# An H3 and SwiGLU block on one core: two groups' FFN activations of the first tokens go through DRAM, their down projection becomes seven products in the second tokens' loop

## Chip, cores and metric

One Trainium2 chip, one of its cores. The metric is the device time of one execution in microseconds (us), the median over runs. The engines are PE (TensorE), DVE (VectorE), ACT (ScalarE), POOL (GpSimd) and SP (SyncE, which here only issues DMAs). All data is float32; matmuls use float32r operands split in a high and a low part.

## The reference

2048 tokens of 512 features. A first half (a gated long convolution with a layer norm and modulation) ends in x; a second half is a SwiGLU feed-forward with 1792 hidden features:

```python
h = layernorm(x) * (1 + ca) + sa
x = x + ga * A(h, k, v, ...)             # short conv, k*v, FFT conv, gate
h = layernorm(x) * (1 + cb) + sb
x = x + gb * ((silu(h @ w_gate) * (h @ w_up)) @ w_down)
```

The change lies in the second half alone.

## The kernel before

**Tokens and features.** x stands in four blocks `xt[0..3]` of 512 tokens each. Blocks 0 and 1 are the first tokens (q = 0), 2 and 3 the second tokens (q = 1). The 1792 hidden features are 14 tiles f of 128; two tiles form a group g (7 groups).

**Gate and up.** For each (q, f), `gate_up` computes gate and up for both blocks at once as a 2 x 2 block product by seven products instead of eight (`seventh`). Each is six matmuls 128x128 by 128x512: two halves of the contraction times three passes (high and low parts). Order of products: 1, 7, 6, 2, 5, 3, 4. They go to PSUM banks a, c and b; bank a takes 1, then 6 on top, then 5, then 3, and ACT copies it out between (p1, p2, r3); bank c takes 7 and 4, b takes 2. So the next six matmuls on a bank wait for the engine that reads it. `gate_up_first` is a variant with another order (1, 5, 7, 2, 3, 6, 4) for the first step of each loop.

**Down.** For q = 0, `down` makes one of eight (block, 128-token) pieces of a group: six matmuls into a bank "dn", and DVE adds it to x. For q = 1, groups 0 to 5 use seven products too (`down_seven`): for two halves i, seven products of three matmuls. The products of one half share three banks (da, db, dc): product 1 goes to da, DVE adds da to x, then product 6 accumulates in da on top, and so on. A product that accumulates therefore waits for DVE's add of the one before. The seven operands come from hidden activations and their sums (`HOP`: A11, S3, S2, A22, A12, S1, S4), each with a high part by ACT and a low part by DVE or POOL (`hi_lo`).

**The order.** Each engine runs its instructions in the order in which the program states them. A loop over n = 2 to 27 (q = n // 14, f = n mod 14) states one `gate_up` after another. Behind its products 1, 7, 6, 2, 5, 3, 4 it calls the functions that tables `AT` and `AT2` (filled by `plan`) list for this step and product, then `feed`, which takes downs from the list `todo`; keys in the tables are product numbers. `late` holds the splits left over from the step before; `finish` states one behind each of the first three products. `SLOTS` is a table of strings that says, allocation by allocation, which buffer or PSUM bank the next tile takes.

**Work around the products in the first loop (n = 2 to 13).** `split_w` makes the seven weight operands of the next f: sums by POOL, high parts by ACT, low parts by POOL; `store_w` writes them to DRAM. `split_wd` scales w_down by gb (DVE, `wd_mul`) and splits it (ACT, POOL). `norm_stats` (DVE), `turn` (DVE 32x32 transposes), `put_rows` and `get_rows` (DMA out and in), `rows_op` and `rows_s` normalise blocks 2 and 3 and turn them so that features lie on the partitions.

**In the second loop (n = 14 to 27).** `reload_w` reads the kept weights back, one f ahead, into a second buffer. `wd_sums` scales w_down and makes its sums, `wd_seven` splits them, both in the odd step of a group.

Of the kernel before, what the change touches and what calls it, by code (L numbers as in the profile page):

```python
# [16 lines left out]
P = 128  # L17
# [25 lines left out]
def adaln_h3_swiglu(ctx, tc, q, k0, v0, kT, vT, ssm, dskip, wgu, wdn, wmod, e_fwd, e_inv, w_c, out):  # L43
# [9 lines left out]
        "e8": "501234671063724603267137537135173135157137157137105637501657305617503657",  # L53
# [3 lines left out]
        "r4": "0123401232040213210432403124031203124013420314201342031420134203142013431202143410201343120",  # L57
        "one": "456723017425036241736412506425173421750621507341573062570634170346250362417364125064251730256731546317027513643105725601341076526370140753623157047561321065745630120376546713025",
# [663 lines left out]
    def split_w(f):  # L722

        st = stage.pop(f)
        a11, a12, a21, a22 = st[:, 0, 0:2], st[:, 0, 2:4], st[:, 1, 0:2], st[:, 1, 2:4]
# [3 lines left out]
        sr = r4([P, 4, 2, P], F32, "sr")  # L729
        pool.tensor_tensor(sr[:, 0], a21, a22, op=ALU.add)  # L730
        pool.tensor_tensor(sr[:, 1], sr[:, 0], a11, op=ALU.subtract)
        pool.tensor_tensor(sr[:, 2], a11, a21, op=ALU.subtract)
        pool.tensor_tensor(sr[:, 3], a12, sr[:, 1], op=ALU.subtract)
        s = e8([P, 2, 4, 2, P], F32R, "wsum")
        act.copy(s[:, 0], sr)
        pool.tensor_tensor(
            w[:, 1, 0:2], st[:, 0].rearrange("p (a k) c -> p a k c", a=2), w[:, 0, 0:2].bitcast(F32), op=ALU.subtract
        )
        pool.tensor_tensor(w[:, 1, 2], a22, w[:, 0, 2].bitcast(F32), op=ALU.subtract)
        for i in (0, 2):  # L740
            pool.tensor_tensor(s[:, 1, i : i + 2], sr[:, i : i + 2], s[:, 0, i : i + 2].bitcast(F32), op=ALU.subtract)
        set_a(f, w, s)
# [3 lines left out]
    def store_w(f):  # L746

        w, s = AOP[f]["t"]
        kept[f] = [dp.tile(list(t.shape), F32, tag=f"{n}{f}", name=f"{n}{f}") for n, t in (("dw", w), ("ds", s))]
        for d, t in zip(kept[f], (w, s)):  # L750
            sp.dma_start(d, t.bitcast(F32))

    def reload_w(f):

        w = ffn["s"].tile([P, 2, 3, 2, P], F32R, tag="wa", name="wa", bufs=2)
        s = e8([P, 2, 4, 2, P], F32R, "wsum")
        for d, t in zip(kept[f], (w, s)):
            sp.dma_start(t.bitcast(F32), d)
        set_a(f, w, s)
# [36 lines left out]
    def wd_sums(g):  # L796

        wd_mul(g)
# [8 lines left out]
        stage["t", g] = tb  # L807

    def wd_seven(g):

        st, tb = stage.pop(("d", g)), stage.pop(("t", g))
        h = D // 2
        b22 = st[:, 1, h:]
        wb, wt = e8([P, 2, 4, h], F32R, "wdb"), e8([P, 2, 4, h], F32R, "wdt")
# [24 lines left out]
    def down(q, g, t, i):  # L839

        parts = 2 if (q, g, t, i) == (1, NG - 1, 0, 3) else 1
        for h in range(parts):
# [9 lines left out]
            if g == NG - 1:  # L852
                sp.dma_start(out[q, :, 4 * t + i, d], xv)
# [8 lines left out]
    SUM = {1: ("a", 0, 0), 7: ("c", 1, 1), 6: ("a", 1, 0), 2: ("b", 0, 0), 5: ("a", 1, 1), 4: ("c", 1, 0), 3: ("a", 0, 1)}  # L862

    def down_seven(g, i, n, bank_):

        k, t, dh = SUM[n]
        a, b = HOP[g][PROD[n][0]], WT[g][PROD[n][1]]
# [9 lines left out]
        xv = xt[2 + t][:, 2 * dh + i]  # L877
        dve.tensor_tensor(xv, xv, o, op=ALU.add)
        if i:
            slots.append(HOP[g].pop(PROD[n][0]))  # L880

    def sevens(g):
        for i in range(2):
            bank_ = {}
            todo.extend(("7", g, i, n, bank_) for n in SUM)

# [131 lines left out]
    def operand(g, n, x, e=dve):  # L1018
        h = HOP.setdefault(g, {})[n] = slots.pop(0)
        hi_lo(h, x, e)  # L1020

    def gate_up(q, f, at):

        def behind(k):
            for fn in at.get(PLACE[k - 1], ()):
                fn()
            feed(k, (q, f) == (0, G + 1))
# [28 lines left out]
        seventh(a, f, 3, True)  # L1056
        sg2 = g2("sg2")
        act.activation(sg2, a, AF.Silu)
        if sv:
# [8 lines left out]
            else:  # L1068
                dve.tensor_tensor(ra[:, 1], sg2, b, op=ALU.mult)
        else:  # L1070
# [4 lines left out]
        seventh(c_, f, 4, True)  # L1075
        dve.tensor_tensor(c_, p2, c_, op=ALU.add)
        dve.tensor_tensor(c_, sg1, c_, op=ALU.mult)
        after(q, f, c_)
# [489 lines left out]
    def release(n):  # L1568
# [31 lines left out]
    def plan(t, *steps):  # L1600
# [5 lines left out]
        (5, 1, turn, 0),  # L1606
        (5, 5, turn, 1),
        (5, 7, turn_rs),
        (5, 3, put_rows, 0),
        (5, 6, put_rs),  # L1610
        (6, 1, turn, 2),
        (6, 7, turn, 3),
        (6, 7, get_rs),
        (6, 3, put_rows, 1),
        (6, 4, get_rows, 0),
        (7, 7, get_rows, 1),
        (7, 6, rows_op, 0, 0, dve),
        (7, 4, rows_op, 1, 0, pool),
        (8, 6, rows_op, 0, 1, pool),
        (8, 6, rows_s, 0),  # L1620
        (8, 4, rows_op, 1, 1, pool),
        (9, 1, rows_s, 1),
# [136 lines left out]
```

## Time and profile before

| | us |
|---|---|
| median of 3 runs | 566.8 (566.38 to 568.26) |
| the profiled execution | 566.24 |
| its span, first to last instruction | 564.5 |
| PE busy | 552.7 |
| DVE busy | 441.5 |
| POOL busy | 317.7 |
| ACT busy | 288.7 |

The first half takes the span's first 154 us or so; the first tokens' loop runs from 173 to 347 us, the second tokens' loop to 555 us. A row of a timeline gives the start, the duration, the engine, the line in the code (always that of a helper here), the operation, result and source tiles, shapes and the count, and in brackets how long the engine stood idle before it and what ended that. A matmul's row counts its pipeline too, so six matmuls show 1.52 us while the next six start 1.36 us later.

### The profile page before, as it was taken

The numbers are of one execution on the slowest core, as the hardware profiler recorded it, in microseconds if no ns is written. First come the engines' busy times: TensorE is split into PE (matmuls) and PEld (weight loads), VectorE is DVE, ScalarE is ACT, GpSimd is POOL, SyncE is SP. The second block draws the span as 40 slices with busy tenths as digits, with TensorE's granted clock in tenths as the row PEclk, the third lists the DMA queues.
The fourth block names the chain that finished last, engine by engine and source line by source line (L and its number), as shares of the span: only waits on it lengthen the run. The fifth ranks groups of instructions, "written<-read, shape, count | busy, mean of one in ns | idle before, by whom it ended". The sixth has DMA issues, their size and how long they took to land.

```text
span 564.5 us, 9861 instructions
## 1 busy us (share of the span) xinstructions
PE 552.7 (98%) x3880; PEld 431.1 (76%) x3880; DVE 441.5 (78%) x602; ACT 288.7 (51%) x444; POOL 317.7 (56%) x298
## 2 busy tenths in 40 slices
PE   9899999898999999999999999999999999999997
PEld 9766456358788888888888888887888888888886
DVE  5989999998889666767567579858686868686766
ACT  3898889734664444434643556243434343434330
POOL 2359746899447966657978667550606061616110
PEclk9999999999999999999999999999999999999999
DMA  8998998991215655982897530544343434343304
GB/s 334 401 406 305 334 245 168 340 240 61 74 43 200 197 199 182 259 263 40 252 334 306 204 131 1 188 182 173 122 160 124 161 127 158 127 165 133 160 1 149
DMA packets 52544, 107.99 MB, mean 191 GB/s; under 512 B 19345, under 2 KB 34065, under 8 KB 46482
## 3 DMA queue, kind: packets, MB, share of 16 engines
q1 hardware_dynamic: 52498, 107.36, 56.3%
q8 instruction: 30, 0.49, 0.4%
q14 instruction: 16, 0.13, 0.1%
HBM read 72.74 MB, written 34.61 MB: 190 GB/s over the span
## 4 chain that ended last, share of the span: by engine, by line
PE 85%; DVE 9%; DMA 3%; ACT 1%; issue 1%; POOL 0%; SPq 0%; ACTq 0%; DVEq 0%
PE a L39 23%; PE dn L39 15%; PE c L39 12%; PE b L39 7%; PE da L39 6%; PE g L39 4%; PE s L39 4%; PE dc L39 3%; PE y L39 3%; DVE xs L39 3%; DVE X L39 2%; PE pk L39 2%; PE iv L39 2%; DMA er<-in_e_fwd 2%; DVE K L39 2%; PE px L39 1%
## 5 line engine op out<-in xcount | busy, mean ns | idle before, releaser
L39 PE MATMUL a<-op,wsum 128*128 128x512 f32 x432 | 109.9, 390 | 0.0
L39 PEld LDWEIGHTS a<-op,wsum 128*128 128x128 f32 x432 | 81.0, 188 | 17.5 <-ACT p L39 0.4
L39 PE MATMUL dn<-wd,acts 128*128 128x512 f32 x336 | 84.8, 389 | 0.0
L39 PEld LDWEIGHTS dn<-wd,acts 128*128 128x128 f32 x336 | 63.1, 188 | 13.1
L39 ACT COPY p<-a 128x512 f32<-128x512 f32 x50 | 29.4, 587 | 57.3 <-PE a L39 57.3
L39 DVE TENSOR_TENSOR x<-x,dn 128x512 f32<-128x512 f32 (+1 forms) x65 | 43.3, 671 | 13.2 <-PE dn L39 12.9
L39 POOL TENSOR_TENSOR wa<-ws,wa 128x512 fp32r<-128x512 f32 (+1 forms) x28 | 32.0, 1164 | 26.6 <-ACT wa L39 26.6
L39 POOL TENSOR_TENSOR tb<-wds 128x256 f32<-128x256 f32 x12 | 8.9, 744 | 62.4 <-DVE wds L39 62.4
L39 DVE TENSOR_TENSOR b<-r,c 128x512 f32<-128x512 f32 x24 | 16.7, 696 | 32.3 <-ACT sg L39 32.3
L39 ACT COPY r<-a 128x512 f32<-128x512 f32 x24 | 14.1, 587 | 53.7 <-PE a L39 53.6
L39 POOL TENSOR_TENSOR wsum<-sr,wsum 128x512 fp32r<-128x512 f32 x28 | 40.1, 1455 | 0.0
L39 PE MATMUL c<-op,wsum 128*128 128x512 f32 x156 | 39.6, 389 | 0.0
L39 PE MATMUL c<-op,wa 128*128 128x512 f32 x156 | 39.6, 389 | 0.0
L39 PE MATMUL b<-op,wa 128*128 128x512 f32 x144 | 36.5, 389 | 0.0
L39 POOL TENSOR_TENSOR wd<-wds,wd 128x512 fp32r<-128x512 f32 x14 | 18.3, 1329 | 30.4 <-ACT wd L39 30.4
L39 PEld LDWEIGHTS c<-op,wsum 128*128 128x128 f32 x156 | 29.3, 188 | 6.1
L39 PEld LDWEIGHTS c<-op,wa 128*128 128x128 f32 x156 | 29.3, 188 | 6.1
L39 POOL TENSOR_TENSOR s<-s,bcs 128x512 f32<-128x512 f32 x26 | 32.9, 1284 | 1.0
L39 DVE TENSOR_TENSOR x<-x,da 128x512 f32<-128x512 f32 x48 | 32.7, 681 | 0.9 <-PE da L39 0.9
L39 PEld LDWEIGHTS b<-op,wa 128*128 128x128 f32 x144 | 27.0, 188 | 5.6
L39 DVE TENSOR_TENSOR xs<-pk,xs 128x1024 f32<-128x1024 f32 x24 | 27.7, 1210 | 2.3 <-PE pk L39 2.2
L39 ACT ACTIVATE sg<-a 128x512 f32<-128x512 f32 x26 | 15.6, 599 | 22.5 <-PE a L39 22.5
(199 smaller groups left out, 1284.5 us busy)
## 6 DMA issues: line engine op xcount, KB each, us to landing
ds<-wsum SPq DMA_DIRECT2D x12, 1024.0 KB, 8.7
wsum<-ds SPq DMA_DIRECT2D x12, 1024.0 KB, 6.4
dw<-wa SPq DMA_DIRECT2D x12, 768.0 KB, 5.8
wa<-dw SPq DMA_DIRECT2D x12, 768.0 KB, 4.4
ws<-in_wgu SPq DMA_DIRECT2D x16, 512.0 KB, 4.3
wds<-in_wdn SPq DMA_DIRECT2D x14, 512.0 KB, 5.0
wm<-in_wmod SPq DMA_DIRECT2D x6, 1024.0 KB, 9.3
away<-X SPq DMA_DIRECT2D x3, 2048.0 KB
```

The source lines that it names most:

```text
L39: return lambda *a, **k: self.tc.keep_in_program_order(f(*a, **k))
```

## The change

For the first tokens, groups 3 and 5 (`LATER`) no longer go through `down` in the first loop. Their activations are written to DRAM (`keep_hidden`), read back in the second loop in the steps of the same group (`hidden`, n = 20, 21 and 24, 25), summed by POOL and split (`hidden_sum`, `hidden_op`), and their down is made by `down_seven` behind that of the second tokens. Those steps take two products behind each seventh, and state them ahead of the step's own DVE operations behind products 2, 5, 3 and 4 (`early`). The first tokens' downs are spread at two a step from n = 6 on.

Since `down_seven` leaves features on the partitions, blocks 0 and 1 are turned as well, with DMAs through DRAM, in n = 15 to 18, and their output is written from there.

To make room, the second loop keeps one copy of the gate and up weights: each operand of the next f is read into the place of the current one as soon as its product is stated. One of the two `wa` buffers holds w_down parts of even groups. In groups 3 and 5 the scaling and splitting of w_down move to the even step. In the first loop `split_w` is cut in three (`split_sum`, `split_a`, `split_s`), with `split_s` behind product 5 from n = 6 on; statistics, turns and row operations of blocks 2 and 3 move one step or more earlier, and their row operations and scaling go from POOL and ACT to DVE. In `SUM` products 4 and 2 change places.

The diff, without the `SLOTS` strings:

```diff
     def turn(t, i):
-        if k == 0:
+        if k == 0 and t < 2 and h:
+            nrm[t, h] = r4([P, NB * 4, 2, 32], F32, "xx")
+        elif k == 0:
             nrm[t, h] = ffn["s"].tile(...)
...
     def rows_s(t, a):
-            act.activation(d, d, AF.Identity, scale=modT[:, 1, b : b + 1], bias=modT[:, 0, b : b + 1])
+            dve.tensor_scalar(d, d, modT[:, 1, b : b + 1], modT[:, 0, b : b + 1], op0=ALU.mult, op1=ALU.add)
...
+    def split_s(f):
+        sr = stage.pop(("s", f))
+        s = e8([P, 2, 4, 2, P], F32R, "wsum")
+        act.copy(s[:, 0], sr)
+        for i in (2, 0):
+            pool.tensor_tensor(s[:, 1, i : i + 2], sr[:, i : i + 2], s[:, 0, i : i + 2].bitcast(F32), op=ALU.subtract)
+        ready(f, "S", s)
...
+    def reload_w(f, *names):
+        w, s = t = AOP[(f - 1) % NF]["t"]
...
+        wb = e8([P, 2, 4, h], F32R, "wdb") if g % 2 else stay[0]
...
-    SUM = {1: ("a", 0, 0), 7: ("c", 1, 1), 6: ("a", 1, 0), 2: ("b", 0, 0), 5: ("a", 1, 1), 4: ("c", 1, 0), 3: ("a", 0, 1)}
+    SUM = {1: ("a", 0, 0), 7: ("c", 1, 1), 6: ("a", 1, 0), 4: ("c", 1, 0), 5: ("a", 1, 1), 2: ("b", 0, 0), 3: ("a", 0, 1)}
+    LATER = (3, 5)
...
+    def keep_hidden(f, t, sg, x):
+        if f not in hid:
+            hid[f] = dp.tile([P, 2, 512], F32, tag=f"h{f}", name=f"h{f}")
+            hsum[2] = r4([P, 2, 512], F32, "hid")
+            dve.tensor_tensor(hsum[2][:, t], sg, x, op=ALU.mult)
+            return
+        dve.tensor_tensor(hsum[2][:, t], sg, x, op=ALU.mult)
+        sp.dma_start(hid[f], hsum[2])
...
-    def feed(k, hold):
-        if hold and k != 5:
+    def feed(k, q, f):
+        if not todo or (q, f) == (0, G + 1) and k != 5:
             return
-        if todo and (todo[0][0] == "7" and k > 1 or k in (2, 3, 4, 5)):
-            downs(2 if todo[0][0] == "7" and k == 5 else 1)
+        if todo[0][0] == "7":
+            if f // G in LATER:
+                downs(2 if (k, f) not in [(1, G * g) for g in LATER if g - 1 not in LATER] else 0)
+            elif k > 1 or todo[0][1] == 0 or len(todo) > 14:
+                downs(2 if k in (1, 5) else 1)
+        elif k in ((), (5,), (2, 5), (2, 4, 5), (2, 3, 4, 5))[4 if q or f < G * LATER[0] else DOWNS[f - G * LATER[0]]]:
+            downs(1)
...
     AT = {
-        (4, 7): lambda: norm_stats(2, range(0, 2)),
-        (4, 6): lambda: norm_stats(2, range(2, 4)),
+        (3, 7): lambda: norm_stats(2, range(0, 2)),
+        (3, 6): lambda: norm_stats(2, range(2, 4)),
...
+    for g in LATER:
+        n0 = NF + G * g
+        for n, k, fn, *a in (
+            (0, 5, hidden), (0, 7, hidden_sum, "S3"), (0, 2, hidden_op, "A11"), (0, 2, hidden_sum, "S1"),
+            (0, 3, hidden_sum, "S2"), (0, 6, hidden_op, "S3", pool), (1, 1, hidden_sum, "S4"),
+            (1, 1, hidden_op, "S2", pool), (1, 1, hidden_op, "A12"), (1, 5, hidden_op, "S1", pool),
+            (1, 5, hidden_op, "A22", pool), (1, 5, hidden_op, "S4", pool), (1, 5, lambda g: sevens(0, g)),
+        ):
+            also(n0 + n, k, fn, g, *a)
     for n in range(G, 2 * NF):
...
+                at[7 if n >= G * LATER[0] else 7].append(lambda nf=nf: split_sum(...))
+                at[7 if n >= G * LATER[0] else 7].append(lambda nf=nf: split_a(...))
+                at[3 if n >= G * LATER[0] else 7].append(lambda nf=nf: split_s(nf))
...
+            for e in range(NG):
+                if n == NF + G * e + (e not in LATER) - (e in LATER and e - 1 in LATER):
+                    if seven(1, G * e):
+                        at[1].append(lambda g=e: wd_sums(g))
+                        at[3].append(lambda g=e: wd_seven(g))
...
-                at[6 if n == G + 1 else 3].append(lambda g=g + 1: split_wd(g))
+                at[6 if n == G + 1 or f >= G * LATER[0] else 3].append(lambda g=g + 1: split_wd(g))
```

More of the change, by code (lines that the diff above doesn't have):

```diff
@@ L728, in split_w, with ready @@
         act.copy(w[:, 0, 2], a22)
[L729 to L736, printed above, removed]
+        e.tensor_tensor(
             w[:, 1, 0:2], st[:, 0].rearrange("p (a k) c -> p a k c", a=2), w[:, 0, 0:2].bitcast(F32), op=ALU.subtract
         )
[L739 to L742, printed above, removed]
+        e.tensor_tensor(w[:, 1, 2], a22, w[:, 0, 2].bitcast(F32), op=ALU.subtract)
+        ready(f, "w", w)
+    def ready(f, k, t):
+        stage[k, f] = t
+        if ("w", f) in stage and ("S", f) in stage:
+            set_a(f, stage.pop(("w", f)), stage.pop(("S", f)))
+    def split_w(f):
+        split_sum(f)
+        split_s(f)
+        split_a(f)
     kept = {}
@@ L750, in store_w, with resplit @@
         for d, t in zip(kept[f], (w, s)):
[L751 to L759, printed above, removed]
+            if t is s or not RESPLIT:
+                sp.dma_start(d, t.bitcast(F32))
+    def reload_w(f, *names):
+        w, s = t = AOP[(f - 1) % NF]["t"]
+        if f not in again:
+            again.add(f)
+            set_a(f, w, s)
+        for n in names:
+            if n[0] == "A" and RESPLIT:
+                i, src = {"A11": (0, wgu[f][:, 0, 0:2]), "A12": (1, wgu[f][:, 0, 2:4]), "A22": (2, wgu[f][:, 1, 2:4])}[n]
+                sp.dma_start(w[:, 1, i].bitcast(F32), src)
+                continue
+            d, x, i = (kept[f][0], w, ("A11", "A12", "A22").index(n)) if n[0] == "A" else (kept[f][1], s, int(n[1]) - 1)
+            sp.dma_start(x[:, :, i].bitcast(F32), d[:, :, i])
+    def resplit(f, n, e=pool):
+        w, i = AOP[f]["t"][0], ("A11", "A12", "A22").index(n)
+        act.copy(w[:, 0, i], w[:, 1, i].bitcast(F32))
+        e.tensor_tensor(w[:, 1, i], w[:, 1, i].bitcast(F32), w[:, 0, i].bitcast(F32), op=ALU.subtract)
+    again = set()
     def set_a(f, w, s):
@@ L807, in wd_sums @@
         stage["t", g] = tb
+    stay = []
     def wd_seven(g):
@@ L813, in wd_seven @@
         b22 = st[:, 1, h:]
-        wb, wt = e8([P, 2, 4, h], F32R, "wdb"), e8([P, 2, 4, h], F32R, "wdt")
+        if g == 0:
+            stay.append(ffn["s"].tile([P, 2, 3, 2, P], F32R, tag="wa", name="wdb0", bufs=2).rearrange("p a n k c -> p a n (k c)"))
+        wb = e8([P, 2, 4, h], F32R, "wdb") if g % 2 else stay[0]
+        wt = e8([P, 2, 4, h], F32R, "wdt")
         act.copy(wb[:, 0, 0:2], st[:, :, :h])
@@ new lines, in hidden, with hidden_sum @@
+    def hidden(g):
+        o = HOP[0, g] = {}
+        for n, fl, t, place in (("A11", 0, 0, 1), ("S1", 0, 1, 0), ("A22", 1, 1, 1), ("A12", 1, 0, 1)):
+            o[n] = slots.pop(0)
+            sp.dma_start(o[n][:, place].bitcast(F32), hid[g * G + fl][:, t])
+    def hidden_sum(g, n):
+        r = {k: v[:, 1].bitcast(F32) for k, v in HOP[0, g].items()}
+        r["A21"] = HOP[0, g]["S1"][:, 0].bitcast(F32)
+        if n == "S3":
+            hsum[0] = r4([P, 2, 512], F32, "hs")
+        if n == "S1":
+            hsum[1] = ffn["s"].tile([P, NB * 4, 2, 32], F32, tag="nn", name="hs", bufs=1).rearrange("p (a b) c d -> p a (b c d)", a=2)
+        x, y, op, at_ = {
+            "S3": ("A11", "A21", ALU.subtract, (0, 0)), "S1": ("A21", "A22", ALU.add, (1, 0)),
+            "S2": ("A22", "S3", ALU.subtract, (0, 1)), "S4": ("A12", "S2", ALU.subtract, (1, 1)),
+        }[n]
+        r["S3"] = hsum[0][:, 0]
+        if n == "S4":
+            r["S2"] = hsum[0][:, 1]
+        pool.tensor_tensor(hsum[at_[0]][:, at_[1]], r[x], r[y], op=op)
+        hraws[n] = hsum[at_[0]][:, at_[1]]
@@ L876, in down_seven, with sevens @@
             )
-        xv = xt[2 + t][:, 2 * dh + i]
+        xv = xt[2 * q + t][:, 2 * dh + i]
         dve.tensor_tensor(xv, xv, o, op=ALU.add)
+        if q == 0 and g == LATER[-1] and n in (2, 5, 4, 3):
+            sp.dma_start(out[0, :, 4 * t + 2 * dh + i], xv)
         if i:
-            slots.append(HOP[g].pop(PROD[n][0]))
-    def sevens(g):
+            slots.append(HOP[q, g].pop(PROD[n][0]))
+    def sevens(q, g):
         for i in range(2):
             bank_ = {}
-            todo.extend(("7", g, i, n, bank_) for n in SUM)
+            todo.extend(("7", q, g, i, n, bank_) for n in SUM)
     def downs(n):
@@ L939, in after @@
     def after(q, f, x):
+        if later(q, f):
+            return
         if not seven(q, f):
@@ L1026, in behind @@
                 fn()
-            feed(k, (q, f) == (0, G + 1))
+            if not ahead_(k):
+                feed(k, q, f)
         g, odd, sv = f // G, f % G, seven(q, f)
@@ L1049, in gate_up @@
         seventh(a, f, 5, True)
+        early(5)
         r3 = g2("r3")
@@ L1069, in gate_up @@
                 dve.tensor_tensor(ra[:, 1], sg2, b, op=ALU.mult)
+        elif later(q, f):
+            keep_hidden(f, 1, sg2, b)
         else:
@@ L1075, in gate_up @@
         seventh(c_, f, 4, True)
+        early(7)
         dve.tensor_tensor(c_, p2, c_, op=ALU.add)
-        dve.tensor_tensor(c_, sg1, c_, op=ALU.mult)
-        after(q, f, c_)
+        if later(q, f):
+            keep_hidden(f, 0, sg1, c_)
+        else:
+            dve.tensor_tensor(c_, sg1, c_, op=ALU.mult)
+            after(q, f, c_)
         behind(7)
@@ L1605, in adaln_h3_swiglu @@
         2,
[L1606 to L1622, printed above, removed]
+        (4, 1, turn, 0),
+        (4, 5, turn, 1),
+        (4, 7, turn_rs),
+        (4, 2, put_rows, 0),
+        (4, 2, put_rs),
+        (4, 3, turn, 2),
+        (5, 1, turn, 3),
+        (5, 1, get_rs),
+        (5, 5, put_rows, 1),
+        (5, 2, get_rows, 0),
+        (5, 6, get_rows, 1),
+        (6, 3, rows_op, 0, 0, dve),
+        (6, 4, rows_op, 1, 0, dve),
+        (7, 1, rows_op, 0, 1, dve),
+        (7, 5, rows_s, 0),
+        (7, 5, rows_op, 1, 1, dve),
+        (7, 7, rows_s, 1),
     )
@@ new lines, in adaln_h3_swiglu @@
+        (6, 4, turn, 1),
+        (6, 4, turn_rs),
+        (7, 1, put_rows, 0),
+        (7, 2, put_rs),
+        (7, 3, turn, 2),
+        (7, 4, turn, 3),
+        (8, 1, put_rows, 1),
+        (8, 6, get_rs),
+        (8, 6, get_rows, 0),
+        (8, 4, get_rows, 1),
+        (9, 4, rows_op, 0, 0, dve),
+        (10, 1, rows_op, 1, 0, dve),
+        (10, 2, rows_op, 0, 1, dve),
+        (10, 4, rows_op, 1, 1, dve),
+        (10, 6, rows_s, 0),
+        (11, 7, rows_s, 1),
+    )
+    plan(
+        1,
+        (NF + 1, 5, turn, 0),
+        (NF + 1, 5, turn, 1),
+        (NF + 1, 7, put_rows, 0),
+        (NF + 1, 7, turn, 2),
+        (NF + 1, 7, turn, 3),
+        (NF + 1, 2, put_rows, 1),
+        (NF + 1, 6, get_rows, 0),
+        (NF + 2, 5, get_rows, 1),
+    )
@@ new lines, in adaln_h3_swiglu @@
+    plan(
+        0,
+        (NF + 1, 4, turn, 0),
+        (NF + 2, 3, turn, 1),
+        (NF + 2, 4, put_rows, 0),
+        (NF + 2, 4, turn, 2),
+        (NF + 3, 5, turn, 3),
+        (NF + 3, 7, put_rows, 1),
+        (NF + 3, 2, get_rows, 0),
+        (NF + 4, 5, get_rows, 1),
+    )
+    for g in LATER:
[7 more added lines that the diff above has]
+            also(n0 + n, k, fn, g, *a)
@@ L1644, in adaln_h3_swiglu @@
     for n in range(G, 2 * NF):
         q, f = n // NF, n % NF
-        at = {k: AT2.get((n, k), []) + ([AT[n, k]] if (n, k) in AT else []) for k in range(1, 8)}
+        at = {k: [] for k in range(1, 8)}
+        if RESPLIT and n >= NF + G:
+            at[7].append(lambda f=f: resplit(f, "A22", none))
+        for k in at:
+            at[k] += AT2.get((n, k), []) + ([AT[n, k]] if (n, k) in AT else [])
         if n + 1 < 2 * NF:
@@ L1650, in adaln_h3_swiglu @@
             if n + 1 >= NF + G:
-                at[1].append(lambda nf=nf: reload_w(nf))
-            else:
-                at[7].append(lambda nf=nf: split_w(nf))
+                for k, names in ((1, ("A11",)), (7, ("S3", "S2")), (2, ("A12",)), (6, ("S1", "S4")), (4, ("A22",))):
+                    at[k].append(lambda nf=nf, names=names: reload_w(nf, *names))
+                if RESPLIT:
+                    at[2].append(lambda nf=nf: resplit(nf, "A11", none))
+                    at[4].append(lambda nf=nf: resplit(nf, "A12", none))
+            else:
+                at[7 if n >= G * LATER[0] else 7].append(lambda nf=nf: split_sum(nf, dve if later(0, nf) and 0 else pool))
+                at[7 if n >= G * LATER[0] else 7].append(lambda nf=nf: split_a(nf, dve if later(0, nf) and 0 else pool))
+                at[3 if n >= G * LATER[0] else 7].append(lambda nf=nf: split_s(nf))
             if n + 2 < NF + G:
@@ L1680, in adaln_h3_swiglu @@
             if seven(q, f):
-                sevens(f // G)
-            else:
+                sevens(1, f // G)
+            elif not later(q, f):
                 todo.extend((q, f // G, t, i) for t in (1, 0) for i in range(4))
```

86 lines of the change are left out of this document (48 added, 38 removed).

## Prediction

> **What bounds the kernel now.** The page comes first: the span and the busy shares.
>
> ```profile
> span 564.5 us, 9861 instructions
> PE 552.7 (98%) x3880; PEld 431.1 (76%) x3880; DVE 441.5 (78%) x602; ACT 288.7 (51%) x444; POOL 317.7 (56%) x298
> ```
>
> PE is busy 98% of the span. That share could still hide slack between matmuls, so the second view is PE's timeline inside the second tokens' loop (columns: start, duration, engine and line, operation, tiles, shape, count). I number the loop's steps n = 2 to 27 (f = n mod 14); the step that starts at 406.49 is n = 18.
>
> ```profile
> 387.31 0.96 PE L39 MATMUL da<-acts,wdt 128*128 128x512 f32 x3 [0.25 <-DVE x L39]
> ...
> 406.49 1.52 PE L39 MATMUL a<-spare,wa 128*128 128x512 f32 x6
> 407.85 1.52 PE L39 MATMUL c<-op,wsum 128*128 128x512 f32 x6
> 409.21 0.84 PE L39 MATMUL da<-op,wdb 128*128 128x512 f32 x3
> 409.89 1.52 PE L39 MATMUL a<-op,wsum 128*128 128x512 f32 x6
> ```
>
> Six matmuls start 1.36 us after the six before them, three 0.68 us: 0.2267 us each, with nothing between. So the price of a matmul is 0.2267 us, and any wait of PE is added to the end. The row at 387.31 shows the only kind of wait this loop has: a product that goes on adding in a PSUM bank (da) waits until DVE has read the partial sum out into x. PE's loops are bound by their own issue; what decides is whether DVE and ACT, each a queue in program order, stay ahead of it.
>
> DVE is the tight one. Its timeline, from the end of n = 17 into n = 18, and one weight scaling later:
>
> ```profile
> 404.68 0.70 DVE L39 TENSOR_TENSOR a<-sg,b 128x512 f32<-128x512 f32 x1 [0.38 <-ACT sg L39]
> ...
> 408.56 0.69 DVE L39 TENSOR_TENSOR c<-p,c 128x512 f32<-128x512 f32 x1
> 409.28 0.69 DVE L39 TENSOR_TENSOR c<-sg,c 128x512 f32<-128x512 f32 x1
> 409.89 0.68 DVE L39 TENSOR_TENSOR x<-x,da 128x512 f32<-128x512 f32 x1
> 410.63 0.69 DVE L39 TENSOR_TENSOR acts<-c,acts 128x512 fp32r<-128x512 f32 x1
> 411.24 0.68 DVE L39 TENSOR_TENSOR x<-x,da 128x512 f32<-128x512 f32 x1
> ...
> 422.36 1.22 DVE L39 TENSOR_TENSOR wds<-wds,bcs 128x1024 f32<-128x1024 f32 x1
> ```
>
> An odd step ends with four DVE operations that include a round trip over ACT (404.68 to 408.56 holds the four and one add: 3.88 less 0.60, 3.3 us). So when the even step n = 18 starts on PE at 406.49, DVE still finishes n = 17: the add at 409.89 is the last of it, four operations later than PE. Back to back, DVE starts one operation every 0.60 to 0.61 us (409.28, 409.89; 410.63, 411.24).
>
> **The change: what PE saves.** For groups 3 and 5 of the first tokens, 8 products of 6 matmuls per group become 14 of 3: 48 to 42, twice: 12 matmuls fewer, 12 x 0.2267 = 2.72 us less. Steps n = 6 to 13 shrink from 66 to 54 matmuls (14.96 to 12.24 us); n = 20 and 24 grow from 63 to 78, n = 21 and 25 to 84, n = 22 and 26 to 69.
>
> **What it costs: DVE in the second loop.** Each moved group brings 14 adds (instead of 8), 2 splits, and its scaling of w_down moves from the odd step to the even one (n = 20, 24), where DVE is late. Work it out on the rows above. At n = 20 there is no product behind the first seventh, two behind the second, then six matmuls, then the third product, which adds in the bank of the first. It is due 1.36 + 1.36 + 2 x 0.68 + 1.36 = 5.44 us after the step's start: 411.93 on the clock of n = 18. DVE after the add at 409.89 does the scaling (from 410.50; the next operation about 1.15 later), the split of A12 (411.65), the add of the first product (412.25 to 412.93). PE goes on at about 413.0: a wait of 1.05 us, at n = 20 and at n = 24. Before, the scaling sat in odd steps (422.36), where the bank has time. If DVE had no lag the cost were 0; if POOL or ACT delays the chain further, up to 1.5.
>
> At the end of n = 21 (and 25), an odd step with two products in every place: from the end T of its third-product matmuls PE does two products, six matmuls, two products, six matmuls, one product: T + 6.12, when the second half's last product wants its bank. DVE ends the first two adds at T + 2.2, spends 3.3 us in the four operations, then adds twice (0.60 + 0.68): T + 6.78. Wait 0.65 us, twice. Queueing the adds ahead of the step's own operations, as the change does in these steps, is already in this count. Sum for the second loop: 2 x (1.05 + 0.65) = 3.4 us.
>
> **What it costs: the first loop.** The statistics of block 2 move from n = 4 to n = 3, the second half in front of the scaling of w_down. Rows of DVE, ACT and PE there:
>
> ```profile
> 198.97 1.22 DVE L39 TENSOR_TENSOR wds<-wds,bcs 128x1024 f32<-128x1024 f32 x1
> ...
> 203.47 0.69 DVE L39 BATCH_NORM_STATS2 bnb<-x 128x6 f32<-128x512 f32 x1
> ...
> 205.09 0.65 DVE L39 TENSOR_TENSOR x<-x,dn 128x512 f32<-128x512 f32 x1
> ```
>
> ```profile
> 200.22 1.05 ACT L39 CAST wd<-wds 128x1024 fp32r<-128x1024 f32 x1 [1.89 <-DVE wds L39]
> 201.17 0.58 ACT L39 COPY p<-a 128x512 f32<-128x512 f32 x1
> ```
>
> ```profile
> 200.26 1.52 PE L39 MATMUL dn<-wd,acts 128*128 128x512 f32 x6
> 201.80 1.66 PE L39 MATMUL a<-op,wsum 128*128 128x512 f32 x6
> ```
>
> The chain is scaling, ACT's cast of it, then behind it on ACT the copy of bank a, for which PE's next six matmuls wait: they were due at 201.62 and started at 201.80, so this chain already touches PE. Half the statistics take 1.62 us (203.47 to 205.09) and now stand in front of the scaling: the whole 1.62 lands on PE. I take 1.65 (bounds 1.4 and 2.2).
>
> Steps 6 to 13 lose 2.7 us each, and what stood in them stays. n = 13 holds three splits of the next tokens' operands:
>
> ```profile
> 332.50 1.52 PE L39 MATMUL a<-op,wa 128*128 128x512 f32 x6
> ```
>
> ```profile
> 340.47 2.22 DVE L39 TENSOR_TENSOR op<-hraw,op 128x1024 fp32r<-128x1024 f32 x1
> ...
> 343.22 0.68 DVE L39 TENSOR_TENSOR b<-p,b 128x512 f32<-128x512 f32 x1
> ...
> 344.75 0.70 DVE L39 TENSOR_TENSOR b<-r,c 128x512 f32<-128x512 f32 x1 [0.27 <-ACT sg L39]
> 345.69 1.23 DVE L39 TENSOR_TENSOR op<-hraw,op 128x1024 fp32r<-128x1024 f32 x1 [0.24 <-ACT op L39]
> ```
>
> ```profile
> 344.12 0.60 ACT L39 ACTIVATE sg<-b 128x512 f32<-128x512 f32 x1
> 344.61 1.05 ACT L39 CAST op<-hraw 128x1024 fp32r<-128x1024 f32 x1
> ```
>
> ```profile
> 311.41 2.54 POOL L39 TENSOR_TENSOR wsum<-sr,wsum 128x512 fp32r<-128x512 f32 x2
> ```
>
> The last six matmuls of n = 13 need b<-r,c done. With two downs fewer ahead they fall due 8 x 1.36 = 10.88 us after the start. DVE loses two adds: b<-p,b starts at 342.62, the sigmoid-gate on ACT ends 1.3 us later, b<-r,c ends at 344.68, which is 12.18 after the start: a wait of 1.35 with the split at 340.47 at 2.22 us, of 0.35 with 1.23 as at 345.69. I take 0.6, nearer to the undisturbed one. The Trainium skill, SBUF — State Buffer, section Who interferes with whom, says that a DVE instruction with two SBUF inputs and a GpSimd instruction that reads SBUF block each other; the row at 340.47 agrees with it, no run here isolates it, and by that rule, with POOL splitting weights at the same place again, the sum would have 1.35 here and the time 0.75 more.
>
> The split of the weight sums now stands behind the operand cast (344.61) on ACT. Undisturbed, the gate starts 9.85 after the start of n = 13, the cast 10.34, the cast of wsum, of the same 128x1024, 11.30 to 12.35, POOL's two differences end 2.55 later, at 14.95, the sum that n = 14 needs for its second product last. That product is due 12.24 + 0.35 + 1.36 = 13.95: wait 1.0 us (0 to 1.2). The four adds and gains of blocks 2 and 3 that move from POOL and ACT to DVE fall in n = 6 to 11, where DVE has two adds fewer a step; 0.1 (0 to 0.7 at n = 7).
>
> **What it costs: transfers.** Blocks 0 and 1 go out and back in n = 15 to 18, and the weights of the next step are reloaded into the one tile just used, in five issues behind five products.
>
> ```profile
> ws<-in_wgu SPq DMA_DIRECT2D x16, 512.0 KB, 4.3
> ```
>
> ```profile
> 234.51 2.75 SPq L39 DMA_DIRECT2D xaway<-n  x4
> ...
> 282.70 8.71 SPq L39 DMA_DIRECT2D x<-xaway  x8
> ```
>
> Worst is n = 15: four 128 KB reads back stand on SP in front of the reload of S1 and S4. Four writes take SP 2.75 us to issue, four reads at most 4.4 (half of 282.70's). The first writes can go when two turns are done, about 5 us into the step; then 2 x 2.75 for both sets of writes, 1.2 for the reloads between them, 4.4 for the reads, 0.8 for S1 and S4: 16.9 us. They land 4.3 later (512 KB), at 21.2, and are needed by the fifth product of n = 16, at 14.96 + 4 x 1.36 + 3 x 0.68 = 22.4. Cost 0, with 1.2 us spare; up to 6 if SP loses that margin in each of n = 15 to 17 by 2 us more. The eight turns on DVE (5 of them in n = 15) fall in steps with four long downs, none of which adds in a bank; 0. The stores of activations and the loads of hidden land 5 us or more before use; 0.
>
> **Sum.** -2.72 + 3.4 + 1.65 + 0.6 + 1.0 + 0.1 = +4.0 us on the profiled execution (566.24, span 564.5): 570.3. The median of the three runs (566.38 to 568.26) is 566.8, 0.56 above the profiled one, so between 570.3 and 570.8; I say 570.5.
>
> **Rivals.** (1) Clean gain, the other side: DVE keeps its lead, all waits above hang on its queue, and PE keeps the whole 2.72: 564.1. The place is the start of n = 20 and 24, and the point is 1.05 us: it decides if DVE ends the first add there by 411.9 on the clock of n = 18 instead of 412.93. For it speaks that the change queues the adds of these steps ahead of the operations that wait for ACT, and that DVE is busy only 78% overall; against it, that from 408.56 to 411.24 DVE's rows show no idle time to give. Chance 0.12. (2) PE catches up: weight loads fill 76% of the span, and if the other 24% were usable, 3.4 us in a step of 14.28, each wait would be made good within its step, 564.1 again. Against it: with nothing to wait for, the groups from 406.49 to 409.89 still start 1.36 and 0.68 apart, as everywhere. Chance 0.05. The Trainium skill, Perfetto Trace Analysis, section Identifying the Most-Contended Engine, would have headroom read from the weight loads' share and not from matmul time; by that rule this rival holds, and the spacing just named disagrees with it. (3) Half the waits: second-loop waits stay and those of n = 4, 13 and 14 shrink, or the reverse: -2.72 + 3.4 = +0.7, 567.5. Chance 0.20. (4) Late reloads, SP held by the reads back: 2 us or more in each of n = 16 to 18 on top: 574 to 577. Chance 0.08. Forecast as summed, 568.5 to 573: 0.55.
>
> **How the numbers follow.** Less than 0.3% (1.7 us) this kernel's measurement can hardly tell from no change: faster is below 565.1, slower above 568.5. Faster 0.17 (rivals 1 and 2), same 0.20 (rival 3), slower 0.63 (forecast and rival 4). The range leaves out most of rivals 1 and 2 and the far part of 4: 565.0 to 574.0; the forecast's own is 568.5 to 573.0.
>
> **What would show it.** In the profile after: PE with 12 matmuls fewer in the loops; rows of PE with idle "<-DVE x" of about 1 us some 5.4 us into n = 20 and n = 24, and 0.65 at the start of n = 22 and 26; about 1.9 us instead of 0.18 ahead of the second a<-op,wsum group of n = 4, behind ACT's copy; 0.6 in n = 13 and 1.0 on the second product of n = 14, behind POOL's wsum. The prediction is wrong if these groups follow each other at 1.36 and 0.68, or if waits on DMA show in n = 15 to 19.

## Result and the profile after

| | before | changed |
|---|---|---|
| median, us | 566.8 (566.38 to 568.26, 4 runs) | 573.5 (573.35 to 575.32, 4 runs) |
| ratio, 95% interval | | 1.0123 (1.0107 to 1.014) |
| the profiled execution | 566.24 | 573.44 |
| its span | 564.5 | 571.6 |

Slower by 1.2%, on the predicted side: the median rose by 6.7 us where 3.7 were forecast. In what follows, one execution of one experiment (588.51 us), which ran in a slower state than the others of its kernel, is left out. The page after begins so:

```profile
span 571.6 us, 10109 instructions
PE 553.7 (97%) x3868; PEld 428.5 (75%) x3868; DVE 461.9 (81%) x627; ACT 284.0 (50%) x440; POOL 336.1 (59%) x309
```

PE has its 12 matmuls fewer (3868 against 3880), and yet the span is 7.1 us longer. The waits of PE (what waited, for what: us in total, times, longest) name where; of these four lines the kernel before has only the third, with 0.2 us:

```profile
PE c L39 <- DVE b L39: 2.2, 2, 1.7
PE a L39 <- POOL rsb L39: 1.7, 1, 1.7
PE da L39 <- DVE x L39: 1.7, 5, 0.5
PE b L39 <- POOL wsum L39: 0.8, 1, 0.8
```

The timeline of PE puts each at its step:

```profile
204.08 1.62 PE L39 MATMUL a<-op,wsum 128*128 128x512 f32 x6 [1.75 <-POOL rsb L39]
...
255.05 1.66 PE L39 MATMUL c<-op,wa 128*128 128x512 f32 x6 [1.73 <-DVE b L39]
...
329.65 1.66 PE L39 MATMUL c<-op,wa 128*128 128x512 f32 x6 [0.52 <-DVE b L39]
...
333.50 1.20 PE L39 MATMUL b<-op,wsum 128*128 128x512 f32 x4 [0.83 <-POOL wsum L39]
...
445.44 0.94 PE L39 MATMUL da<-acts,wdt 128*128 128x512 f32 x3 [0.21 <-DVE x L39]
...
460.49 0.98 PE L39 MATMUL da<-acts,wdb 128*128 128x512 f32 x3 [0.49 <-DVE x L39]
```

They lie in n = 4, 7, 13, 14, 21 and 22 (25 and 26 repeat the last two). The brackets give less than each costs, because PE's records count its pipeline. I add up start to start instead: the distance between the starts of two matmuls that follow each other, less 0.2267 us, called excess below. I sum it over all matmuls that are late. From n = 2 on it is 2.1 us before and 11.7 after. The second matmul behind a wait starts 0.11 us late as well, so that a wait of 0.65 costs 0.76.

| place | forecast, us | excess gained, us |
|---|---|---|
| 12 matmuls fewer | -2.72 | -2.72 |
| n = 4 | 1.65 | 1.7 |
| n = 7 | 0.1 | 2.0 |
| n = 13, its second and its last product | 0.6 | 1.1 |
| n = 14 | 1.0 | 1.1 |
| second loop, n = 20 to 26 | 3.4 | 3.5 |
| n = 2, 8 | 0 | 0.2 |
| sum | 4.0 | 6.9 |

The rest to the 7.1 us of the spans lies outside: n = 2 starts 0.45 later (173.45 against 173.00), and the end behind the last matmul is about 0.2 shorter. The change does not touch the first half, and in the profiles of all kernels shown here n = 2 starts anywhere from 172.56 to 174.54 us: spans and medians carry this spread, the excess does not (part of it is a stretch of lower clock, shown in the last section). n = 15 to 19 have no excess beyond that of before: the turns, the transfers and the late reloads cost nothing.

### The profile page after: what moved, and what is told of

Its sections match the earlier page's. It is cut to its first block, busy times and chain, and to the rows that moved or that the text cites. A ratio compares the mean times of both kernels' runs of the same rounds, so it can differ in the third digit from the quotient of the medians.

```text
span 571.6 us, 10109 instructions
## 1 busy us (share of the span) xinstructions
PE 553.7 (97%) x3868; PEld 428.5 (75%) x3868; DVE 461.9 (81%) x627; ACT 284.0 (50%) x440; POOL 336.1 (59%) x309
## 4 chain that ended last, share of the span: by engine, by line
PE 69%; DVE 16%; DMA 5%; POOL 3%; ACT 3%; issue 3%; SPq 1%; DVEq 0%; ACTq 0%; POOLq 0%
PE a L39 18%; PE dn L39 9%; PE c L39 8%; PE da L39 6%; PE b L39 5%; PE g L39 4%; PE s L39 3%; PE y L39 3%; DVE xs L39 3%; PE dc L39 3%; DVE x L39 2%; DVE X L39 2%; PE pk L39 2%; PE iv L39 2%; DVE hraw L39 2%
## 5 line engine op out<-in xcount | busy, mean ns | idle before, releaser
L39 PE MATMUL dn<-wd,acts 128*128 128x512 f32 x240 | 60.4, 389 | 0.0
L39 PEld LDWEIGHTS dn<-wd,acts 128*128 128x128 f32 x240 | 45.0, 188 | 9.4
L39 DVE TENSOR_TENSOR x<-x,da 128x512 f32<-128x512 f32 x64 | 43.4, 680 | 5.4 <-PE da L39 5.3
L39 POOL TENSOR_TENSOR wsum<-sr,wsum 128x512 fp32r<-128x512 f32 x28 | 36.6, 1328 | 17.6 <-ACT wsum L39 17.6
L39 POOL TENSOR_TENSOR wa<-ws,wa 128x512 fp32r<-128x512 f32 (+1 forms) x28 | 35.9, 1303 | 17.4 <-ACT wa L39 17.4
L39 DVE TENSOR_TENSOR x<-x,dn 128x512 f32<-128x512 f32 (+1 forms) x49 | 32.5, 668 | 7.2 <-PE dn L39 6.9
L39 POOL TENSOR_TENSOR sr<-ws 128x256 f32<-128x256 f32 x28 | 24.9, 888 | 6.7 <-issue 6.7
L39 DVE TENSOR_TENSOR x<-x,dc 128x512 f32<-128x512 f32 x32 | 21.8, 683 | 8.2 <-PE dc L39 7.8
```

What stands on the lines that cost most here:

```text
L39: return lambda *a, **k: self.tc.keep_in_program_order(f(*a, **k))
```

## Experiments

My theory: PE is bound by its own issue, and every added microsecond is a wait made by the order in the queues of DVE, ACT and POOL, in n = 7 by DVE operations that POOL lengthens. Rivals: transfers, or waits that come back elsewhere when one is taken away.

**The statistics (n = 4).**

```diff
-        (3, 6): lambda: norm_stats(2, range(2, 4)),
+        (3, 4): lambda: norm_stats(2, range(2, 4)),
```

> The changed kernel with the statistics' second half of block 2 behind the last product of n = 3 instead of ahead of the scaling of w_down. Theory (order on POOL, ACT and DVE at the end of n = 3 makes PE wait for rsb's product in n = 4): the wait of 1.9 us of PE in n = 4 goes, the step's excess over 0.2267 us a matmul falls from 2.0 to 0.3-0.5, the time by 1.4 to 1.8 us. Rival (the wait comes from the turned blocks' transfers, not from the place of the statistics): the wait stays, time within 0.3 us of the changed kernel's.

The reverse, the kernel before with the move of the statistics alone:

```diff
-        (4, 7): lambda: norm_stats(2, range(0, 2)),
-        (4, 6): lambda: norm_stats(2, range(2, 4)),
+        (3, 7): lambda: norm_stats(2, range(0, 2)),
+        (3, 6): lambda: norm_stats(2, range(2, 4)),
```

> The kernel before with one part of the change: the statistics of block 2 move from n = 4 to n = 3, no hidden products moved, no block turned. Theory: n = 4 gets the wait of 1.6 to 1.9 us, the time is 1.3 to 1.8 us above that of the kernel before. Rival (the wait needs the turned blocks too): within 0.3 us of the kernel before.

The kernel before with that move took 568.35 us (567.52 to 569.5), ratio 1.0031 (1.002 to 1.0043): 1.9 us more. Its PE timeline:

```profile
203.83 1.66 PE L39 MATMUL a<-op,wsum 128*128 128x512 f32 x6 [1.65 <-ACT p L39]
```

This one move makes the whole wait, with no block turned and no product moved. The row also settles who is waited for. In the changed kernel the bracket said POOL's rsb, but rsb only ended last there, some 0.1 us behind ACT's copy of p; here the same wait, of the same size, is put down to the copy, as the prediction's chain has it.

In the changed kernel with the statistics behind the last product, the excess in n = 4 falls from 2.0 to 0.7, not quite to the 0.3 to 0.5 expected (the kernel before has 0.3). Yet the median is 572.7 (571.88 to 573.64), ratio 1.0107 (1.0092 to 1.0121): only 0.8 less. Its profiled execution shows why. PE's timeline behind the wait in n = 7:

```profile
252.88 1.83 PE L39 MATMUL c<-op,wa 128*128 128x512 f32 x6 [1.77 <-DVE b L39]
254.50 2.77 PE L39 MATMUL a<-op,wa 128*128 128x512 f32 x6
257.06 1.81 PE L39 MATMUL c<-op,wsum 128*128 128x512 f32 x6
```

Six matmuls take 2.56 us (254.50 to 257.06), 0.427 each in place of 0.2267. The stretches ahead, in and behind it (the share behind POOL's busy time is the granted TensorE clock):

```profile
249.00:252.60 3.60, 2.11 (x10) 1.41 (x8) 2.94 (x6) 1.17 (x3) 0.95 (x1) 1.00 0.93 369
252.60:257.60 5.00, 4.72 (x14) 3.76 (x15) 4.96 (x7) 1.78 (x3) 2.53 (x2) 0.66 0.48 197
257.60:262.00 4.40, 4.40 (x21) 3.62 (x20) 1.76 (x3) 0.99 (x3) 4.05 (x5) 1.00 0.81 196
```

A granted clock of 0.66 over 5.0 us is half the clock for some 3.4 of them; eight matmuls 0.2 us longer each make 1.6 us. In the changed kernel's profile the same wait at 255.05 has nothing of the kind behind it:

```profile
254.50:260.00 5.50, 4.95 (x22) 4.10 (x23) 5.46 (x7) 2.26 (x4) 2.54 (x2) 1.00 0.55 225
```

Some executions pay it and others not. The mean clock tells whether an execution had such a stretch, though not where (the last section shows one in the first half). Here the two executions at 1.0 have spans of 569.8 and 570.0, the three at 0.997 of 570.8 to 571.9, against 571.1 to 571.6 for the three of the changed kernel at 0.999 or 1.0. At equal clock the move is worth 1.1 to 1.8 us.

**The row operations (n = 7).**

```diff
-        (7, 5, rows_op, 1, 1, dve),
-        (7, 7, rows_s, 1),
+        (8, 5, rows_op, 1, 1, dve),
+        (8, 7, rows_s, 1),
```

> The changed kernel with block 1's row operation and row sum moved from n = 7 to n = 8. Theory (DVE's two added row operations, each lengthened beside POOL's sums, push the add that frees b behind PE): the wait of 1.7 us at the end of n = 7 goes, 1.5 to 2.0 us less. Rival 1 (n = 8 has no more room than n = 7, its 48 matmuls take 10.9 us): the wait comes back in n = 8 or 9, time within 0.5 us of the changed kernel's. Rival 2 (the transfers of the rows are late): n = 7's wait stays.

571.49 us (570.67 to 572.46), ratio 1.0086 (1.0073 to 1.0099): 2.0 less. PE has no excess in n = 7, 8 or 9, so n = 8, whose 54 matmuls take 12.24 us, did have the room. That does not tell too many operations from lengthened ones, so next POOL was made quiet in n = 7 (this kernel leaves out the sums and low parts of weight tile f = 8, so it no longer computes the block):

```diff
+        if f == 8:
+            for i in range(4):
+                e.memset(sr[:, i], 0.0)
+            return
         e.tensor_tensor(sr[:, 0], a21, a22, op=ALU.add)
...
+        if f == 8:
+            e.memset(w[:, 1].bitcast(F32), 0.0)
+            ready(f, "w", w)
+            return
```

> The changed kernel in which POOL, in n = 7, only writes constants where it works out the sums and low parts of weight tile f = 8 (those are left out; all PE and DVE work stays). Theory (collision of DVE with POOL): DVE's operations of two SBUF inputs at 243 to 253 us fall from 1.73-2.31 us to 1.2-1.3, the wait of PE for b at the end of n = 7 falls from 1.73 us to under 0.4, the time by 1.4 to 2 us. Rival (the length of DVE's queue alone, without the collision): DVE's durations fall by under 0.2 us each and the wait stays above 1.2 us.

DVE and POOL in the changed kernel, one timeline each:

```profile
243.84 1.74 DVE L39 TENSOR_TENSOR hraw<-x,bcs 128x1024 f32<-128x1024 f32 x1
...
246.23 1.73 DVE L39 TENSOR_TENSOR hraw<-hraw,bcs 128x1024 f32<-128x1024 f32 x1
247.99 1.30 DVE L39 TENSOR_SCALAR hraw<-hraw,modT 128x512 f32<-128x512 f32 x2
249.21 2.31 DVE L39 TENSOR_TENSOR hraw<-hraw,bcs 128x1024 f32<-128x1024 f32 x1
...
254.30 0.70 DVE L39 TENSOR_TENSOR b<-r,c 128x512 f32<-128x512 f32 x1 [0.66 <-ACT sg L39]
```

```profile
244.58 1.60 POOL L39 TENSOR_TENSOR sr<-sr,ws 128x256 f32<-128x256 f32 x1
...
246.83 1.72 POOL L39 TENSOR_TENSOR sr<-ws,sr 128x256 f32<-128x256 f32 x1
249.15 2.97 POOL L39 TENSOR_TENSOR wa<-ws,wa 128x512 fp32r<-128x512 f32 x2 [0.60 <-ACT wa L39]
```

The same DVE operations with POOL only writing:

```profile
243.54 1.22 DVE L39 TENSOR_TENSOR hraw<-x,bcs 128x1024 f32<-128x1024 f32 x1
...
245.39 1.19 DVE L39 TENSOR_TENSOR hraw<-hraw,bcs 128x1024 f32<-128x1024 f32 x1
246.62 1.00 DVE L39 TENSOR_SCALAR hraw<-hraw,modT 128x512 f32<-128x512 f32 x2
247.53 1.22 DVE L39 TENSOR_TENSOR hraw<-hraw,bcs 128x1024 f32<-128x1024 f32 x1
...
251.53 0.70 DVE L39 TENSOR_TENSOR b<-r,c 128x512 f32<-128x512 f32 x1 [0.67 <-ACT sg L39]
```

The queue holds the same DVE operations in the same order. The three of two SBUF inputs shrink from 1.74, 1.73 and 2.31 us to 1.22, 1.19 and 1.22; b<-r,c starts 2.77 us earlier (2.5 of it behind the first of them), and PE waits nowhere in n = 7: excess 0, span 569.3 against 571.6, median 572.31 (571.04 to 572.89), ratio 1.0096 (1.008 to 1.0113). The median is 1.2 less than that of the changed kernel, not the 1.4 to 2 expected; the rows are clearer. So the wait was the collision: without it the same operations fit into n = 7. The rule that the prediction quoted from the Trainium skill, SBUF — State Buffer, section Who interferes with whom (a DVE instruction with two SBUF inputs and a GpSimd instruction that reads SBUF block each other, while one that only writes does not), agrees with this run, at 0.5 to 1.1 us an operation. Only the first of the three ran beside POOL's writes (243.45 to 245.19 us) and was as short as the other two, which ran beside an idle POOL.

**n = 13 and 14.**

```diff
-        (13, 5): lambda: diff("B11", "B22", "B11"),
+        (13, 6): lambda: diff("B11", "B22", "B11"),
...
-                at[3 if n >= G * LATER[0] else 7].append(lambda nf=nf: split_s(nf))
+                late_s = at[3 if n >= G * LATER[0] else 7]
+                late_s.insert(0 if n == NF - 1 else len(late_s), lambda nf=nf: split_s(nf))
...
-        for i in (2, 0):
+        for i in (0, 2) if f == 0 else (2, 0):
```

> The changed kernel with the order at n = 13 and 14 changed: B11's difference behind product 6 instead of 5, the low parts of weight tile f = 0 placed ahead of B22's cast, and the low part that PE needs first made first. Theory (queue order on DVE, ACT and POOL): the waits of 0.8 us at the end of n = 13 and 1.0 us in n = 14 go, 1.3 to 1.9 us less. Rival (reloads through the SP queue hold the operands at the start of the second tokens): the waits stay.

Both waits are gone: the products at these two places follow each other at 1.36 us, and the excess falls from 11.7 to 9.8, that is by the two places. The quarter microsecond at the second product of n = 13 stays. The median is 573.23 (571.81 to 573.82), ratio 1.011 (1.0089 to 1.0131): 0.3 less, not the 1.3 to 1.9 expected. In the profile, n = 2 starts at 174.14, 0.7 later than in the changed kernel. The four executions have spans of 568.9 and 570.4 at clocks of 0.999 and 1.0, and 571.0 and 571.3 at 0.996 and 0.997; so the median alone would have missed what the rows show. No reload held anything up.

**The second loop.** First, the scaling of w_down for groups 3 and 5 on DVE, where the prediction had it:

```diff
-        wd_mul(g, pool if g in LATER else dve)
+        wd_mul(g)
```

> The changed kernel with the scaling of w_down for groups 3 and 5 on DVE instead of POOL. Theory (the step of the prediction, for the kernel that it took this to be): at n = 20 and 24 PE waits 0.8 to 1.3 us more for the third product's place, 1.5 to 2.5 us slower in all than the changed kernel. Rival (DVE has room, POOL was the late one): POOL's low part of S1 comes earlier, the waits of 0.3 us go, and the time is the same or 0.5 us less.

574.9 us (574.5 to 576.02), ratio 1.0146 (1.0126 to 1.0166): 1.4 more than the changed kernel. PE and DVE in n = 20:

```profile
427.58 0.96 PE L39 MATMUL da<-acts,wdt 128*128 128x512 f32 x3 [0.86 <-DVE x L39]
```

```profile
425.11 1.22 DVE L39 TENSOR_TENSOR wds<-wds,bcs 128x1024 f32<-128x1024 f32 x1
...
426.85 0.68 DVE L39 TENSOR_TENSOR x<-x,da 128x512 f32<-128x512 f32 x1
```

Start to start the wait is 1.02 us, plus 0.11, at n = 20 and again at n = 24. The prediction's working (1.05) holds for this kernel. But the changed kernel runs the scaling on POOL, and there PE waits less, for another thing: its row and, behind it, S1's low part:

```profile
422.09 2.41 POOL L39 TENSOR_TENSOR wds<-wds,bcs 128x1024 f32<-128x1024 f32 x1
...
427.48 1.30 POOL L39 TENSOR_TENSOR acts<-raw,acts 128x512 fp32r<-128x512 f32 x1
```

The operation ends at 428.78; the second matmul of the product that uses it starts at 428.84 instead of 428.60, 0.24 us late. In n = 21 it is another queue: the low part of A12 on DVE waits for ACT's cast, and DVE's adds for PE stand behind it (the row of PE at 445.44 above):

```profile
441.59 1.31 DVE L39 TENSOR_TENSOR op<-op 128x512 fp32r<-128x512 f32 x1 [1.10 <-ACT op L39]
```

Three orders of this loop at once (one string of `SLOTS` changes with them):

```diff
-                        at[1].append(lambda g=e: wd_sums(g))
+                        at[7 if e in LATER else 1].append(lambda g=e: wd_sums(g))
...
-            (1, 1, hidden_op, "S2", pool), (1, 1, hidden_op, "A12"),
+            (1, 1, hidden_op, "S2", pool), (1, 5, hidden_op, "A12"),
...
-                dve.tensor_tensor(ra[:, 1], ra[:, 1], a, op=ALU.add)
+                if g not in LATER:
+                    dve.tensor_tensor(ra[:, 1], ra[:, 1], a, op=ALU.add)
...
         early(7)
+        if sv and odd and g in LATER:
+            dve.tensor_tensor(ra[:, 1], ra[:, 1], a, op=ALU.add)
```

> The changed kernel with three orders of the second loop changed: the scaling of w_down for groups 3 and 5 behind the last product of n = 20 and 24 instead of product 1; A12's cast behind product 5; the add of 5a' stated behind the early adds. Theory (queues of POOL and DVE set the waits of n = 20 to 22 and 24 to 26, 4.1 us together): 2 to 3.5 us less, each even step back to under 0.3 us of excess. Rival (PE waits for transfers of the kept activations): these steps keep over 3 us of excess. A third outcome: POOL's work moved behind product 7 is late for n = 21 and costs 1 us or more there.

578.99 us (577.47 to 581.71), ratio 1.0212 (1.0185 to 1.0239): the third outcome, worse than expected. The waits at the start of n = 22 and 26 are gone. So are the short ones behind S1's low part: without the scaling ahead of it, POOL starts it 4.7 us into n = 20 instead of 7.5, and the excess of n = 20 and of n = 24 falls from 0.6 to 0.2.

```profile
425.91 1.30 POOL L39 TENSOR_TENSOR acts<-raw,acts 128x512 fp32r<-128x512 f32 x1 [2.57 <-ACT acts L39]
```

But n = 21 has a wait of 1.73 us and one of 0.68 behind it, and n = 25 one of 5.2. PE, DVE and POOL in n = 25:

```profile
520.93 1.62 PE L39 MATMUL da<-acts,wdt 128*128 128x512 f32 x3 [5.04 <-DVE x L39]
```

```profile
514.76 5.43 DVE L39 TENSOR_TENSOR acts<-acts 128x512 fp32r<-128x512 f32 x1 [1.61 <-POOL hs L39]
520.11 0.67 DVE L39 TENSOR_TENSOR x<-x,da 128x512 f32<-128x512 f32 x1
```

```profile
514.67 2.53 POOL L39 TENSOR_TENSOR acts<-hs,acts 128x512 fp32r<-128x512 f32 x2
517.15 1.27 POOL L39 TENSOR_TENSOR op<-op 128x512 fp32r<-128x512 f32 x1
518.37 1.27 POOL L39 TENSOR_TENSOR op<-hs,op 128x512 fp32r<-128x512 f32 x1
```

POOL, started later, runs four operations without a pause from 514.67 to 519.64. A DVE operation of a form that takes 0.68 us elsewhere starts 0.09 us after the first of them and ends 0.55 us after the last. DVE's adds for PE stood behind it. A stretch of half clock follows this wait too (granted clock 0.50 from 521 to 525 us).

The same kernel without the moved scaling:

> The changed kernel with two of the three orders of the second loop: A12's cast behind product 5, the add of 5a' behind the early adds; the scaling of w_down stays where the change has it. Theory (these two hold DVE up at n = 21 and 22, and 25 and 26; the earlier run was slower for the moved scaling alone): the waits of 0.65 us at the start of n = 22 and 26 and of 0.38 us in n = 21 and 25 go, 1.6 to 2.2 us less than the changed kernel. Rival (the moved casts are late in turn on POOL and ACT): waits of 0.4 us or more at dc's products of n = 21 and 25, as in that earlier run, and less than 0.7 us gained.

571.49 us (570.51 to 573.22), ratio 1.0079 (1.0058 to 1.0101): 2.0 less than the changed kernel. The waits of 0.65 and 0.38 are gone and dc's products have none, so it was the moved scaling that spoilt the run before. The two orders were moved together; which of them cures which wait is read from the rows, not tested.

**All together.** With all three orders of the second loop:

> The changed kernel with the statistics behind the last product, the rows of block 1 in n = 8, the orders at n = 13 and 14, and those of the second loop all changed as above, the computation as in the changed kernel. Theory (waits add up on PE and are independent): the sum of the single gains, 6 to 9 us, so 564.5 to 567.5 us: level with the kernel before or up to 0.4% faster. Rival (a wait taken away comes back at the next point): over 568.5 us.

571.11 us (569.41 to 577.34), ratio 1.0096 (1.0062 to 1.0131); the rival's outcome, by the moved scaling: n = 25 again has a DVE operation of 5.4 us and a wait of 4.8. Without it:

> The changed kernel with the statistics behind the last product, the rows of block 1 in n = 8, the orders at n = 13 and 14, and the two orders of the second loop, the scaling of w_down left where the change has it. Theory (12 matmuls fewer are 2.72 us, and the rest of the difference is made of waits that each has its own place): total excess of PE over 0.2267 us a matmul 2.7 to 3.5 us from n = 2 on against 2.1 in the kernel before, so 1.4 to 2.1 us less than the kernel before, 564.6 to 565.4 us; and no stretch of half clock in the loops, since no wait over 0.6 us is left. Rival (other costs of the change remain, by transfers or by more DVE and POOL work): level with the kernel before or slower, over 566.5 us.

565.5 us (564.93 to 566.65) against 566.56 of the kernel before beside it, ratio 0.9976 (0.9965 to 0.9987). Its page, and the one loop wait that PE has left:

```profile
span 563.8 us, 10110 instructions
```

```profile
PE da L39 <- DVE x L39: 0.2, 1, 0.2
```

The excess is 4.2 us, more than the 2.7 to 3.5 expected. Above the kernel before stand 0.4 in n = 4, 0.3 in n = 13, 0.4 to 0.5 in each of n = 20 and 24 for S1's low part, and 0.2 in each of n = 2, 22 and 26; so the time is at the upper edge, 0.1 above. The account closes: 12 matmuls fewer, -2.72, and 2.1 more excess than before make -0.6 us; the spans differ by 0.7. The clock was 1.0 in all twelve executions. Taken away one at a time, the waits gave 1.3 (statistics), 2.1 (rows), 1.9 (n = 13 and 14) and 2.1 us of excess (adds), 7.4 in all; together they gave 7.5. So none of these came back elsewhere.

## Why the prediction was right, and where it was off

**Price of a matmul, and the gain.** Right: the account of the last experiment closes with 2.72 us, less the excess that is left. Rivals 1 to 3 fall: PE made up for no wait, though the weight loads fill only 75%, and the waits of n = 4, 13 and 14 and the sum of the second loop all came at about their forecast size.

**n = 4.** Right: 1.65 against 1.7, by the chain named (statistics, scaling, cast, copy of p), shown from both sides.

**n = 7.** The step that failed: "The four adds and gains ... 0.1 (0 to 0.7 at n = 7)". It is 2.0 us, two thirds of the miss of 2.9 in the sum. The operations were counted as if undisturbed and set against two adds fewer a step; but they have two SBUF inputs and were moved beside POOL's sums. The prediction had a row of this, 2.22 against 1.23 us at 340.47, used it in n = 13 and nowhere else.

**n = 13 and 14.** Queues and sign right. At the end of n = 13, 0.8 us came instead of 0.6, but not by the price that the 0.6 was weighed from: the split of 2.22 us ran undisturbed (1.21), and another operation fell beside POOL, a difference (hraw<-hraw) that took 1.72 instead of 1.22:

```profile
319.88 1.72 DVE L39 TENSOR_TENSOR hraw<-hraw 128x1024 f32<-128x1024 f32 x1
...
326.36 1.21 DVE L39 TENSOR_TENSOR op<-hraw,op 128x1024 fp32r<-128x1024 f32 x1
```

That the size is close is partly luck. n = 14 cost 1.1 for 1.0. The quarter microsecond at the second product of n = 13, behind POOL's wsum, was not foreseen.

**Second loop.** The total is right (3.5 for 3.4), its make-up half. The 0.65 at n = 22 and 26 is there to the digit (0.49 in the bracket, 0.65 start to start). The 1.05 at n = 20 and 24 is not: the scaling was put on DVE, while the changed kernel says `wd_mul(g, pool if g in LATER else dve)`, a line that the diff above does not show. What stands there instead, 0.4 to 0.5 us gained in each of n = 20, 21, 24 and 25 behind POOL's low part and behind A12's cast on ACT, was not foreseen and adds up to 1.9 us, about as much as 2 x 1.05. This agreement is chance.

**Transfers.** Right at 0: rival 4 falls with n = 15 to 19.

## What to carry to other kernels

When work is moved onto DVE or POOL, price it by the rows in which both run beside each other: the price is what the other engine does in that place, not the operation. Read from the diff on which engine each moved operation runs, before counting that engine's queue. And take waits away one at a time: whatever is left of them comes off the 2.72 us (with 2.1 us left the span gained 0.7, the median 1.1). Read single gains of 1 to 2 us from the profile's rows, since the clock and the start of the loop move the median by as much.

## What the hardware showed that was not expected

- **Half clock behind a wait.** After waits of PE of 1.9 us (n = 7, statistics moved) and 5.2 us (n = 25, moved scaling), start to start, PE issued a 128x512 matmul every 0.427 us, for 8 to 10 matmuls. The same wait of n = 7 in the changed kernel's own profile was followed by full speed. The Trainium skill, TensorE: Matmul & The Clock Gate, section What's actually happening, has the clock halved after an idle window of about 3.4 us that runs free of the program: the length of the stretch at n = 7 (about 3.4 us) agrees, and so does the chance in it, but a wait of 1.9 us was enough, and the stretch behind n = 25 is longer (granted clock 0.50 from 521 to 525 us, ten matmuls). The change is not needed for it either. Four profiles (rows in n = 8, scaling on DVE, three orders, adds' order) have such a stretch in the first half, behind waits of 1.5 and 0.5 us that the changed kernel's own profile has too, at full clock. The same matmuls, first with the rows in n = 8 (granted clock 0.57 from 143 to 147 us), then in the changed kernel:

```profile
142.93 8.47 PE L39 MATMUL g<-op,wg 128*128 128x512 f32 x29 [0.53 <-POOL op L39]
```

```profile
143.42 6.90 PE L39 MATMUL g<-op,wg 128*128 128x512 f32 x29 [0.54 <-POOL op L39]
```

The kernel before has a mean clock of 0.996 or 0.997 in 11 of its 47 executions beside these runs; that its stretches lie in the same place is likely, but none of them was profiled. What decides is open.

- **DVE held off by several POOL operations in a row.** 5.43 us for an operation of 0.68, past four operations of POOL, and 5.44 in the run with all orders. The pairs in n = 7 cost 0.5 to 1.1 us. Why POOL kept its turn four times in the one place was not tried.
